# A corrected port flag in the planner of an attention and two-mixer kernel, and a new list of nudges that re-deals its order

## The chip, the cores and the metric

The kernel runs on one core of one Trainium2 chip. A time is the device time of one execution in microseconds (us). The time of a kernel is the median of several executions. The profile shows one execution, instruction by instruction, with the engines PE (TensorE; PEld is its weight load), DVE (VectorE), ACT (ScalarE), POOL (GpSimd) and SP (the queue that issues nearly all DMAs).

## The reference

For 4 batches of 12 heads, 448 tokens and head size 64, the reference computes an attention, a gated mixer and a second mixer, one after the other:

```python
q_n, k_n = (rmsnorm(q, g_q), rmsnorm(k, g_k))
attn = softmax(q_n @ k_n.T / 8); x = attn @ v            # per head, then heads side by side: [4, 448, 768]
h = np.maximum(x @ w_in, 0.0)                            # 768 -> 1024
u, v = h[..., :512], h[..., 512:]
v_s = np.einsum('ts,bsd->btd', w_spatial, norm(v)) + b_spatial[None, :, None]
x = (u * v_s) @ w_out                                    # 512 -> 768
u = x + (np.maximum(x.T @ w_tok1, 0.0) @ w_tok2).T       # over tokens, 448 -> 256 -> 448
out = u + np.maximum(u @ w_ch1, 0.0) @ w_ch2             # 768 -> 1536 -> 768
```

## The kernel before, in words

The program doesn't write its instructions in the order in which they are issued. It first records them. `Plan.add` (from L162) makes an `Op` of every call, with an estimated cost, with the operations it depends on, and with a flag `port`: True where the planner holds that the operation occupies what VectorE and GpSimd share. `Plan.place` is a list scheduler. It walks through time, takes for each engine the waiting operation of the lowest weight, refuses an operation whose flag `port` is set while the other engine's flagged operation runs, prefers TensorE products of the tiling in use over those of another (tilings are 1: contraction over at most 64 rows, 2: at most 64 output rows, 0: neither), and gives PSUM banks to tiles. `Plan.issue` calls it eight times with weights from a backward pass and keeps the best. Then it changes these weights by a long list of seeds, `NUDGES` (L473): every seed moves the weights of a stretch of operations up or down by a pseudo-random amount. The order that comes out is issued (L464 is the line on which all recorded operations are issued, so most rows of the profile bear it). `Plan.warmers` puts throwaway products into a planned TensorE stall of over `IDLE` = 1500 ns (L456).

The work, by the names in the profile:

- Attention goes over 24 pairs of heads. For a pair: `raw` (q and k as loaded, scaled on GpSimd or VectorE by the root mean squares `r...`), `tp` (transposes on TensorE, of `raw`, of the exponentials `e` and of `stage`, a spatial weight), `whole` or `qt`, `kt` (transposed q and k in SBUF), `sc` (scores), `nm` (VectorE's row maxima), `e` (ScalarE's exponentials), `et` (the transposed exponentials, copied from PSUM by ScalarE and VectorE), `av` (the values' product, 64 output rows), `over` (reciprocals of the row sums, which go through DRAM, `over_d`), and `xp`, the pair's result in two parts (upper on ScalarE, rest on GpSimd).
- The first mixer goes over the 4 batches, each after its 6 pairs: `vps` (weights `wv`), `ups` (weights `wu`, written to DRAM once as `wu_d` and loaded again, 768 KB at a time), `sps` (spatial), `xps`.
- The second mixer: `h1ps` and `u_ps` over tokens, then `h2ps` and `o_ps` over channels, each a long row of products.
- Weights come as 64-bit words and are converted on ScalarE, VectorE and GpSimd (`word`, `wpart`).

The first batch's attention has to run before any mixer product is there. Later attention pairs run among mixer products.

Of the kernel before, what the change touches and what calls it, by code (L numbers as in the profile page):

```python
# [152 lines left out]
class Plan:  # L153
# [8 lines left out]
    def add(self, engine, fn, args, kwargs):  # L162
        op = Op()
        op.engine, op.more, op.dma = engine, [], fn == "dma_start"
        op.call = (fn, args, kwargs)
        named = dict(kwargs)
        out = named.pop("out", None)
        rest = list(args)
        if out is None:
            out = rest.pop(0)  # L170
        outs = [x for x in (out, named.pop("accum_out", None)) if isinstance(x, Part)]
        ins = [x for x in rest + list(named.values()) if isinstance(x, Part)]
        op.cost, op.late = self.estimate(engine, fn, out, ins, kwargs)

        sbuf = [x for x in ins if not x.tile.psum]
        op.port = engine == "gpsimd" and bool(sbuf) or engine == "vector" and (
            len(sbuf) > 1 and free(sbuf[1].shape) > 1
            or len(ins) == len(sbuf) and fn in ("tensor_scalar", "tensor_copy"))

        op.parts = 0  # L180
        if engine == "tensor":
            op.parts = 1 if ins[0].shape[0] <= 64 else 2 if out.shape[0] <= 64 else 0
        if self.joined:
            self.joined[0].more.append(op)
            self.joined[0].cost += op.cost
            op = self.joined[0]
        else:
            op.deps = set()
            self.ops.append(op)
        if self.joined is not None:  # L190
            self.joined.append(op)
        for x in ins:
            t = x.tile
            assert t.writers, "read before it is written"
            assert t.make or covered(x, t.writers), "read before all of it is written"
            op.deps.update(w for y, w in t.writers if x.meets(y))
            if t.psum:
                op.deps.update(r for _, r in t.readers if r.engine != engine)
            t.readers.append((x, op))
            t.users.append(op)  # L200
        for x in outs:
            t = x.tile
            before = [w for y, w in t.writers if x.meets(y)]
            if not before:
                self.later.append((op, t.after))
            op.deps.update(before)
            op.deps.update(r for y, r in t.readers if x.meets(y))
            t.writers = [(y, w) for y, w in t.writers if not x.covers(y)] + [(x, op)]
            t.readers = [(y, r) for y, r in t.readers if not x.covers(y)]
            t.users.append(op)  # L210
        op.deps.discard(op)
# [259 lines left out]
SWITCH, NEAR, FAR, EARLY = 300, 2500, 10000, 95000  # L471
NUDGED = 4000
NUDGES = (  # L473
# [21 lines left out]
)  # L495
ENGINES = "gpsimd", "scalar", "sync", "tensor", "vector"
IDLE, SPARE, PACE = 1500, 200, 546
# [33 lines left out]
def covered(x, writers):  # L531

    left = volume(x.box)
    for y, _ in writers:
        left -= volume([(max(a, c), min(b, d)) for (a, b), (c, d) in zip(x.box, y.box)])
    return left <= 0
# [9 lines left out]
def free(shape):  # L546
    n = 1
    for x in shape[1:]:
        n *= x
    return n  # L550
# [11 lines left out]
def attention_moe_mixer(  # L562
# [887 lines left out]
    def up(wp, chan, ut):  # L1450
# [4 lines left out]
        for name, k in PRODUCTS:  # L1455
            w = chan.pop(k, None) or build(wp, c1_d, k)
            for b in range(B // 2):
                op = operand(wp, [P, 2, JH, S], "op", 2, first[b][name])
                for f in range(KH):
# [12 lines left out]
                    if name == "A11":  # L1472
                        nc.scalar.activation(at0(c12), ps, AF.Copy)
                    elif name == "A12":
                        add(c11, c12)
                        relu(c11)
                    elif name == "S2":
                        add(c12, c12)
                    elif name == "S3":
                        add(c21, c12)  # L1480
                    elif name == "S1":
                        add(c22, c21)
                        add(c12, c12)
                        relu(c22)
                    elif name == "S4":
                        add(c12, c12)
                        relu(c12)
                    else:
                        add(c21, c21, ALU.subtract)
                        relu(c21)  # L1490
# [186 lines left out]
```

## Time and profile before

| what | value |
|---|---|
| median of 3 executions | 847.92 us (847.16 to 848.81) |
| the profiled execution's own time | 847.23 us |
| its span, first to last instruction | 845.2 us |
| PE busy | 833.1 us (99%), 5530 records |
| DVE / ACT / POOL busy | 674.7 / 526.7 / 344.6 us |

Some 2.0 us of the time lie around the span. A "busy" PE includes time in which a product streams or drains and the modelled end of a product, so idle PE time by the profile is a lower bound of what TensorE loses. A product of 32-bit numbers leaves two records for one instruction (5530 records for 5255 instructions).

### The profile page before, as it was taken

How to read it: one execution, taken by the hardware profiler on the slowest of the kernel's cores; microseconds unless marked ns; L12 is line 12 of the kernel's file. 1: busy time of each engine (PE TensorE's matmuls, PEld its weight loads, DVE VectorE, ACT ScalarE, POOL GpSimd, SP SyncE). 2: the span in 40 equal slices, each digit the busy share in tenths (PEclk: the TensorE clock that was granted, in tenths of full speed). 3: DMA queues.
4: the chain of work that ended last, by engine and by line, in shares of the span. 5: the costliest groups of instructions: out<-in, count | busy, mean ns of one | idle time of the engine just before them, and what ended most of it. 6: DMA issues, size and time to landing. Idle time of an engine off the chain costs nothing.

```text
span 845.2 us, 16488 instructions
## 1 busy us (share of the span) xinstructions
PE 833.1 (99%) x5530; PEld 700.4 (83%) x5530; DVE 674.7 (80%) x1340; ACT 526.7 (62%) x1268; POOL 344.6 (41%) x431
## 2 busy tenths in 40 slices
PE   7999999999999999999999999999999999999998
PEld 5454567777678876787799999999999999999998
DVE  6899899886787778787475677988889876998863
ACT  6999899897776878766343565554345654343331
POOL 2457555663445524242152222525331018515460
PEclk9999999999999999999999999999999999999999
DMA  6656676766765866466968787667555635742441
GB/s 170 161 160 185 177 232 184 236 169 170 241 184 144 216 171 196 124 180 194 331 201 247 234 275 252 220 197 221 156 175 175 214 123 161 226 140 84 140 142 66
DMA packets 158532, 157.94 MB, mean 187 GB/s; under 512 B 79216, under 2 KB 141616, under 8 KB 158448
## 3 DMA queue, kind: packets, MB, share of 16 engines
q1 hardware_dynamic: 157984, 156.86, 62.1%
q8 instruction: 44, 0.72, 0.4%
q14 instruction: 40, 0.33, 0.1%
q10 hardware_dynamic: 464, 0.03, 0.0%
HBM read 117.95 MB, written 38.88 MB: 186 GB/s over the span
## 4 chain that ended last, share of the span: by engine, by line
PE 82%; ACT 9%; DMA 3%; DVE 3%; issue 1%; SPq 1%; POOL 0%; ACTq 0%; POOLq 0%; DVEq 0%
PE o_ps L464 18%; PE h2ps L464 18%; PE xps L464 7%; PE ups L464 7%; PE av L464 6%; PE vps L464 5%; PE tp L464 5%; PE sc L464 4%; PE sps L464 4%; ACT e L464 4%; PE h1ps L464 4%; PE u_ps L464 3%; ACT et L464 2%; ACT sq L464 1%; DMA raw<-in_k_dram 1%
## 5 line engine op out<-in xcount | busy, mean ns | idle before, releaser
L464 PE MATMUL h2ps<-op,w 128*128 128x448 f32 x756 | 154.1, 366 | 0.0
L464 PEld LDWEIGHTS o_ps<-w,op 128*128 128x128 f32 x900 | 154.0, 188 | 0.0
L464 PE MATMUL o_ps<-w,op 128*128 128x384 f32 (+1 forms) x900 | 153.9, 332 | 0.0
L464 PEld LDWEIGHTS h2ps<-op,w 128*128 128x128 f32 x756 | 141.6, 188 | 11.2
L464 ACT ACTIVATE e<-sc,nm 112x448 f32<-112x448 f32 x184 | 121.7, 692 | 5.5 <-DVE nm L464 5.3
L464 DVE TENSOR_REDUCE nm<-sc 112x1 f32<-112x448 f32 x192 | 110.2, 615 | 8.0 <-PE sc L464 7.3
L464 ACT ACTIVATE op<-c 128x768 fp32r<-128x768 f32 x49 | 41.5, 847 | 83.7 <-PE o_ps L464 77.3
L464 POOL TENSOR_TENSOR src<-src 128x384 f32<-128x384 f32 x48 | 61.2, 1284 | 73.4 <-DMA src<-c_d 56.1
L464 PEld LDWEIGHTS tp<-ident,e 64*128 64x128 f32 (+2 forms) x1120 | 55.5, 139 | 27.4 <-ACT e L464 9.5
L464 ACT ACTIVATE et<-tp 128x448 f32<-128x448 f32 (+1 forms) x144 | 72.7, 560 | 4.9 <-PE tp L464 4.5
L464 DVE TENSOR_SCALAR word<-word 128x256 f32<-128x256 f32 (+5 forms) x132 | 60.5, 462 | 18.4 <-ACT word L464 17.3
L464 DVE SCALAR_TENSOR_TENSOR word<-raw,word 128x256 uint32<-128x256 uint32 (+2 forms) x132 | 71.2, 541 | 1.8
L464 POOL TENSOR_TENSOR u<-u,o 128x384 f32<-128x384 f32 x28 | 40.5, 1464 | 68.4 <-ACT o L464 38.9
L464 PE MATMUL tp<-ident,e 48*128 48x48 f32 (+2 forms) x1120 | 65.4, 232 | 1.2 <-ACT e L464 0.8
L464 PE MATMUL ups<-xp,wu 128*128 128x448 f32 x288 | 65.9, 368 | 0.0
L464 DVE TENSOR_TENSOR op<-c,op 128x768 fp32r<-128x768 f32 x49 | 54.6, 1115 | 10.3 <-ACT op L464 10.3
L464 PE MATMUL av<-et,v 128*64 128x448 f32 x288 | 61.1, 550 | 1.4 <-ACT e L464 0.9
L464 PEld LDWEIGHTS ups<-xp,wu 128*128 128x128 f32 x288 | 53.7, 188 | 6.4 <-ACT e L464 0.7
L464 DVE TENSOR_TENSOR c<-c,h2ps 128x448 f32<-128x448 f32 x84 | 49.7, 613 | 8.4 <-PE h2ps L464 8.2
L464 PE MATMUL xps<-wo,g 128*128 128x384 f32 x288 | 55.1, 340 | 0.0
L464 PE MATMUL sc<-kt,qt 64*112 64x448 f32 x384 | 52.9, 384 | 0.0
L464 PE MATMUL vps<-wv,xp 128*128 128x512 f32 x216 | 52.8, 397 | 0.0
(146 smaller groups left out, 1595.1 us busy)
## 6 DMA issues: line engine op xcount, KB each, us to landing
src<-c_d SPq DMA_DIRECT2D x132, 192.0 KB
wu<-wu_d SPq DMA_DIRECT2D x16, 768.0 KB
wo<-wo_d SPq DMA_DIRECT2D x16, 768.0 KB
raw<-in_moe_w_ch_dram SPq DMA_DIRECT2D x36, 256.0 KB
raw<-in_moe_w_ch_dram SPq DMA_DIRECT2D x24, 384.0 KB
raw<-in_q_dram SPq DMA_DIRECT2D x48, 112.0 KB
over<-over_d SPq DMA_DIRECT2D x48, 112.0 KB
u<-u_d SPq DMA_DIRECT2D x28, 192.0 KB
```

The lines of the kernel that those rows point to most:

```text
L464: getattr(getattr(self.nc, op.engine), fn)(*args, **kwargs)
```

## The change

It alters which operations carry the flag `port`: a VectorE `tensor_tensor` of two SBUF operands now carries it however short its second operand is, and a `tensor_scalar` or `tensor_copy` from SBUF of one element per partition no longer does. It replaces the list `NUDGES` by another, of 267 seeds in place of 228. No operation is added, removed or moved to another engine, and `IDLE`, `SPARE` and `PACE` of the throwaway products stay as they are.

```diff
-            len(sbuf) > 1 and free(sbuf[1].shape) > 1
-            or len(ins) == len(sbuf) and fn in ("tensor_scalar", "tensor_copy"))
+            len(sbuf) > 1 and (fn == "tensor_tensor" or free(sbuf[1].shape) > 1)
+            or len(ins) == len(sbuf) and fn in ("tensor_scalar", "tensor_copy") and free(ins[0].shape) > 1)
...
 NUDGES = (
-    30000007, 30000023, 30000034, 30000042, 30000052, 30000053, 30000068, 30000070, 30000077, 30000078, 30000083,
...
+    30000003, 30000004, 30000005, 30000028, 30000030, 30000033, 30000039, 30000046, 30000048, 30000053, 30000066,
...
 )
 ENGINES = "gpsimd", "scalar", "sync", "tensor", "vector"
 IDLE, SPARE, PACE = 1500, 200, 546
```

What it does to the order, at three places. First TensorE, where the eighth pair's `raw` is transposed, shortly ahead of the first mixer product. Before:

```order
L464 MATMUL av<-et,v_864 64x448 x2
L464 MATMUL tp<-ident,raw 128x112 x8
L464 MATMUL tp<-ident,stage 128x112 x3
L464 MATMUL sc<-whole 112x448 x2
L464 MATMUL tp<-ident,stage 64x112
L464 MATMUL av<-et,vrest 64x448 x2
L464 MATMUL av<-et,v_1125 64x448 x2
```

And now:

```order
L464 MATMUL av<-et,v_952 64x448 x4
L464 MATMUL av<-et,vrest 64x448 x2
L464 MATMUL tp<-ident,e 128x112
L464 MATMUL tp<-ident,raw 128x112 x4
L464 MATMUL tp<-ident,e 128x112 x2
L464 MATMUL tp<-ident,raw 128x112
L464 MATMUL tp<-ident,stage 128x112 x3
L464 MATMUL tp<-ident,raw 128x112 x3
L464 MATMUL tp<-ident,e 128x112 x4
```

The eight transposes of `raw`, which stood in one row, are split by transposes of `e` and `stage`.

Second TensorE again, around the first mixer products `vps` and the values' product `av` that follows them. Before:

```order
L464 MATMUL vps<-wv,xp 128x512 x7
L464 MATMUL tp<-ident,e 128x112 x7
L464 MATMUL sc<-whole 112x448 x2
L464 MATMUL tp<-ident,raw 128x64 x14
L464 MATMUL sc<-whole 112x448 x2
L464 MATMUL av<-et,v_1310 64x448 x6
L464 MATMUL vps<-wv,xp 128x512 x12
```

And now:

```order
L464 MATMUL vps<-wv,xp 128x512 x8
L464 MATMUL tp<-ident,e 128x112 x7
L464 MATMUL vps<-wv,xp 128x512 x8
L464 MATMUL tp<-ident,raw 128x64 x14
L464 MATMUL sc<-whole 112x448 x4
L464 MATMUL av<-et,v_1321 64x448 x4
L464 MATMUL sc<-whole 112x448 x4
L464 MATMUL vps<-wv,xp 128x512 x6
```

Six of the twelve `vps` that stood behind the `av` (5 + 7 were ahead of it, 2 + 8 + 8 are now) have moved ahead of it.

Third the DMA queue SP, at the first load of `wu`, which the first `ups` reads. Before (the queue's row 98 is the load):

```order
L464 DMA raw<-in_k_dram 64x64
L464 DMA raw<-in_k_dram 64x7x64
L464 DMA raw<-in_k_dram 64x6x64
L464 DMA wu<-wu_d_59 128x1536
L464 DMA raw<-in_moe_w_in_dram 128x2x256
L464 DMA wu_d_60<-wpart 256x1x256
```

And now (row 143):

```order
L464 DMA v_1666<-in_v_dram 128x3x64
L464 DMA wu_d_62<-wpart 256x1x256
L464 DMA vrest<-in_v_dram 64x64 x2
L464 DMA wu<-wu_d_59 128x1536
L464 DMA raw<-in_moe_w_out_dram 128x512
L464 DMA v_1666<-in_v_dram 128x3x64
L464 DMA wu_d_62<-wpart 256x1x256
L464 DMA wu<-wu_d_60 128x1536
```

The first load of `wu` now stands behind two writes of the third part of `wu_d` and just ahead of the second load, where it had stood 42 rows ahead of that one.

## Rows read from the trace of the kernel before

**Rows 1.** The page's head, its busy times, and the clock line of its 40 slices.

```profile
span 845.2 us, 16488 instructions
...
PE 833.1 (99%) x5530; PEld 700.4 (83%) x5530; DVE 674.7 (80%) x1340; ACT 526.7 (62%) x1268; POOL 344.6 (41%) x431
...
PEclk9999999999999999999999999999999999999999
```

**Rows 2.** Busy times by stretches: stretch, its length, busy us and records by engine, clock, DMA.

```profile
0.00:21.13 21.13, 15.82 (x98) 12.25 (x99) 12.88 (x33) 13.77 (x34) 6.30 (x24) 1.00 0.69 170
...
21.13:84.52 63.39, 60.33 (x363) 31.70 (x361) 57.44 (x131) 63.39 (x183) 37.26 (x59) 1.00 0.62 169
84.52:126.78 42.26, 41.57 (x278) 25.06 (x278) 38.23 (x104) 36.69 (x105) 22.09 (x34) 1.00 0.70 205
126.78:824.07 697.29, 697.17 (x4681) 613.33 (x4678) 559.32 (x1065) 410.33 (x947) 279.00 (x317) 1.00 0.63 192
...
824.07:845.20 21.13, 18.20 (x118) 18.03 (x117) 6.84 (x11) 2.55 (x3) 0.00 (x0) 1.00 0.19 66
```

**Rows 3.** Pieces of the chain that ended last: start us, us, what, records.

```profile
406.88 14.97 PE vps L464 x66
...
537.30 151.19 PE h2ps L464 x746
688.49 153.79 PE o_ps L464 x900
```

**Rows 4.** Waits of the weight load: who waited for whom, us, times, longest.

```profile
PEld av L464 <- issue: 30.6, 125, 0.7
...
PEld tp L464 <- issue: 8.6, 20, 1.3
PEld sc L464 <- issue: 5.7, 19, 0.7
```

**Rows 5.** Groups of ACT: shapes, count, busy us, mean ns of one, idle before.

```profile
L464 ACT ACTIVATE et<-tp 128x448 f32<-128x448 f32 x96 | 55.5, 592 | 3.8 <-PE tp L464 3.6
...
L464 ACT ACTIVATE xp<-over 128x448 fp32r<-128x448 f32 x24 | 15.2, 635 | 10.7 <-DVE over L464 10.6
...
L464 ACT ACTIVATE ry<-ra 128x14 f32<-128x14 f32 x16 | 3.6, 227 | 2.0 <-POOL ra L464 1.9
L464 ACT ACTIVATE ry<-ry 128x14 f32<-128x14 f32 x16 | 3.6, 227 | 0.4
```

**Rows 6.** Timeline of PE, 83 to 104 us: start us, us, what [idle before <-releaser].

```profile
83.59 0.60 PE L464 MATMUL tp<-ident,raw 112*128 112x112 f32 x4 [0.73 <-POOL raw L464]
84.59 0.60 PE L464 MATMUL tp<-ident,raw 112*128 112x112 f32 x4 [0.40 <-POOL raw L464]
...
94.68 1.39 PE L464 MATMUL vps<-wv,xp 128*128 128x512 f32 x5
...
98.58 1.01 PE L464 MATMUL sc<-whole 64*112 64x448 f32 x4
...
101.34 2.48 PE L464 MATMUL av<-et,v 128*64 128x448 f32 x12 [0.53 <-DVE over L464]
```

**Rows 7.** Loads of `wu` on SP, the first long `ups`, and the DMA of 112 to 125 us.

```profile
80.06 0.61 SPq L464 DMA_DIRECT2D wu<-wu_d  x1
...
115.31 0.61 SPq L464 DMA_DIRECT2D wu<-wu_d  x1
...
131.19 3.62 PE L464 MATMUL ups<-xp,wu 128*128 128x448 f32 x17
...
DMA packets 3026, 3.27 MB, mean 251 GB/s; under 512 B 1920, under 2 KB 2391, under 8 KB 3025
```

**Rows 8.** Throwaway products at the start, by stretches; and PE's longest wait for data.

```profile
1.60:5.20 3.60, 3.60 (x17) 3.60 (x18) 1.00 0.78 171
5.50:6.90 1.40, 1.40 (x15) 1.40 (x14) 1.00 0.70 144
...
9.37 0.60 PE L464 MATMUL tp<-ident,raw 112*128 112x112 f32 x4 [1.60 <-DVE raw L464]
```

44 rows, old and new, of the table NUDGES are left out of this document.

## The prediction
> **What bounds the kernel now.** I read the page first, then the busy times by stretches, then the chain of waits, then the places where TensorE waited. The page says that PE is busy for 833.1 of 845.2 us [rows 1], so 12.1 us of the span hold no product. The stretches say where those lie [rows 2]: 21.13 - 15.82 = 5.31 us in the first 21 us, 63.39 - 60.33 = 3.06 us from 21 to 85 us, 42.26 - 41.57 = 0.69 us from 85 to 127 us, 697.29 - 697.17 = 0.12 us in the 697 us after that, and 21.13 - 18.20 = 2.93 us in the last slice. The reader is to see that from 127 us on TensorE never stops. The second mixer alone is a row of 746 products `h2ps` in 151.19 us, then 900 `o_ps` in 153.79 us, without a gap in the chain [rows 3]. So the kernel is bound by TensorE's work, and an order can only win what lies ahead of 127 us.
>
> From 21 to 85 us a second engine is full: ACT is busy for 63.39 of 63.39 us [rows 2]. There the first pairs' exponentials feed the transposes and value products, and no mixer product can fill in, since `vps` needs the first batch's results. What ScalarE must do ahead of the first `vps` bounds this stretch from below; TensorE's idle 3.06 us are its echo.
>
> **The change, part by part.** *The flags.* No instruction reads them; they act through the order alone. Their direct cost is nothing and nothing has to hide it.
>
> *The work.* Counted in the two orders, every engine issues the same instructions: 5255 on TensorE in both, 1342 on VectorE, 1084 on ScalarE, 433 on GpSimd, 883 on SP. The throwaway products are 16, 1 and 4 in both, at the same three places, so that part of the planner's pass fills nothing new. Cost: 0.
>
> *The ends.* TensorE's first 80 products and its last 1651 stand in the same order in both. The 5.31 us of the first slice and the 2.93 us of the last stay: 0.
>
> *Changes of tiling on TensorE.* I counted in the orders how often a product of one tiling follows one of another: 136 times before and 136 times now. The mix differs: from column tiling to full products 13 before and 5 now, from half rows to full 32 and 38, from column tiling to half rows 24 and 30, the opposite of the last 22 and 20, full to half rows 30 and 28, full to columns 15 and 15. The rows price a stop of the weight load for no visible cause by the product that comes next: 30.6/125 = 0.245 us for `av`, 8.6/20 = 0.43 us for `tp`, 5.7/19 = 0.30 us for `sc` [rows 4]. If all 12 switches that changed kind moved from the cheapest to the dearest, that is 12 x (0.43 - 0.245) = 2.2 us, and as much the other way if they moved back. I take 0, since the total is the same and the rows name the next product, not the kind of switch; 2.2 us either way stays as a bound. The Trainium skill, page "TensorEngine Tiling (Array Packing)", section "Key Properties", says that changing the tiling mode drains TensorE, whichever mode; by that rule 136 switches against 136 cost the same and this term is 0, where the rows would allow 2.2 us.
>
> *ScalarE's work ahead of the first mixer product.* 391 products stand ahead of the first `vps` in both orders. The last exponential that a transpose needs just ahead of it has 184 ACT operations in front of it in both. They differ by four: one more `et` (0.592 us) and one more `xp` (0.635 us), two `ry` fewer (2 x 0.227 us) [rows 5]. That is 0.592 + 0.635 - 0.454 = +0.77 us. ScalarE is full there, so I take all of it; the other end is 0, since PE idles 3.06 us in the stretch and part of the wait can move into that.
>
> *The transposes of the eighth pair.* Before, they waited 0.73 and 0.40 us for GpSimd's scaled `raw`, one half each [rows 6]. Now the second half's first transpose has two transposes of `e` ahead of it, at about 0.1 us each, which cover 0.2 us of the 0.40 us; the first half still follows the value products directly, with one transpose between. GpSimd's row is as before (a `wpart` product, then the two scalings). I take -0.2 us; the ends are -1.13 us (both waits gone) and +0.4 us (GpSimd later by half a scaling).
>
> *The value product behind the first `vps`.* It waited 0.53 us until VectorE had emptied the earlier one's bank [rows 6]. Now six more `vps`, at 14.97/66 = 0.227 us [rows 3], and two more `sc` of the pair that took 1.01 us for two (four records) [rows 6] stand between the two value products: 1.4 + 1.0 us against 0.53 us. The wait goes, -0.53 us. If VectorE's copy is later by as much, it stays: 0.
>
> *SP.* The first load of `wu` stood at row 98 of the queue and stands at row 143. Before, it was issued at 80.06 us for use at 131.19 us; the second load, at row 140 then, was issued at 115.31 us [rows 7]. So the first load will be issued at about 115 us, with some 16 us in hand, and at the stretch's mean rate of 251 GB/s [rows 7] its 768 KB take 3.1 us. Cost 0, covered by the products ahead of the first `ups` (617 before, 599 now); without that cover it is the second rival.
>
> Sum against the profiled execution's own 847.23 us: + 0.77 - 0.2 - 0.53 = +0.04, that is **847.3 us**. The profiled execution lies 0.7 us under the median of the three shown (847.92 us) and inside their range, so I leave the forecast at 847.3 us. It is no change. 0.2% of the time, 1.7 us, is about what a measurement of this kernel can tell from none, so "the same" reaches from 846.2 to 849.6 us.
>
> **The rivals.** *First, the idle time ahead of 127 us goes.* The new order may close half or all of the 3.06 + 0.69 us [rows 2]: 847.3 - 1.9 = 845.4 us at half, 847.3 - 3.75 = 843.6 us at all. For it speaks that both places which I compared have more work in front of the wait. Against it speaks that ACT is full from 21 to 85 us and has as much to do as before ahead of the first `vps`; a wait that TensorE is spared there comes back a few products later. I give it 0.34.
>
> *Second, slower: the first load of `wu` comes too late.* It stands now behind two writes of `wu_d` that wait for GpSimd's `wpart`, and right ahead of the second load. If the queue is held for more than about 16 - 3 = 13 us (less where other loads share the engines, by half the rate 16 - 6 = 10 us), the 18 first `ups` wait, and from there each us is one us of the kernel, less what other products are ready. With 3 us over, that is 850.3 us. Against it: SP issued what stood there at 115 us. Chance 0.11.
>
> *Third, slower: the saturated stretch gets holes.* From 127 us to the end of the attention pairs, ahead of the long row of `vps` at 407 us [rows 3], TensorE lost at most 0.12 us [rows 2]; there the old order has nothing left to win, and a new one can lose. At the rate of the stretch before (0.69 us in 42.26 us) over 280 us, that is 4.6 us; half of it gives 849.6, two thirds 850.3 us. It decides where a batch's mixer products run out before the next batch's pairs are done. Chance 0.11.
>
> *Fourth, the clock.* The granted clock is 1.00 (2.4 GHz) in all 40 slices [rows 1], through a wait of 1.60 us [rows 8] as well, so fewer idle stretches can give no clock back. At the start the products ran slower, 17 in 3.60 us and then 15 in 1.40 us [rows 8], though the column reads 1.00 there too; if a longer idle brought that pace back for as many products, it cost 17 x (3.60/17 - 1.40/15) = 2.0 us: 849.3 us. The Trainium skill, page "TensorE: Matmul & The Clock Gate", section "Why this matters for your kernels", says that a TensorE left idle between bursts falls back to the lower clock; by it a new order could lose time that the old one keeps, and the trace has no stretch that did. Chance 0.04.
>
> That the change doesn't do what it says has in part happened already (no more throwaway products than before), and its time is that of the forecast.
>
> **How the numbers follow.** The forecast has 0.40, and the clock's 0.04 ends within 0.2% too: 0.44 for the same. Faster is the first rival, 0.34. Slower are the second and third, 0.22. The range leaves out about a tenth on each side: it goes into the first rival as far as four fifths of the idle time, 844.3 us, which also holds the 2.2 us of the switches, and up to the two slower rivals' 850.3 us.
>
> **What would show it.** Right: ACT again full from 21 to 85 us and PE idle there 2 to 4 us; the first `vps`, at 94.68 us before [rows 6], between 94 and 96 us; no wait of the value product that follows the first `vps`; PE idle under 0.5 us from 127 us on; the row of 746 `h2ps` starting within 1 us of 537.3 us [rows 3]. The first rival would show as PE idle under 1.9 us between 21 and 127 us, with the first `vps` earlier than 94 us. The second would show as `ups` waiting for a DMA at about 130 us, the third as waits of PE between 127 and 400 us, the fourth as a slice with a lower clock or with products at the doubled interval. Most likely to make the forecast wrong is that small waits inside what counts as busy add up: a tenth of a us at each of the 136 switches is 13.6 us, more than all the idle time that the profile shows.

## The result, and the profile after

The changed kernel takes 852.60 us (median of 8 executions, 849.79 to 855.17), the kernel before 848.01 us beside it (8, 847.16 to 849.67). The ratio is 1.0053, 95% interval 1.0036 to 1.0070: slower by 4.5 us, between 3.1 and 5.9. The forecast was 847.3 us, with a range up to 850.3 us.

The profiled execution took 853.08 us, 5.85 us more than the one before, so it shows about 1.3 us more than the medians differ by. The page's head and busy times, to be set beside [rows 1]:

```profile
span 851.3 us, 16447 instructions
...
PE 834.1 (98%) x5530; PEld 701.6 (82%) x5530; DVE 679.2 (80%) x1340; ACT 527.8 (62%) x1268; POOL 347.8 (41%) x431
```

The span is 6.1 us longer. PE is busy 1.0 us longer and idle 851.3 - 834.1 = 17.2 us instead of 12.1 us, 5.1 us more. Where, the busy times by stretches tell (stretch, its length, busy us and records of PE, PEld, DVE, ACT, POOL, then clock, DMA share and GB/s), beside [rows 2]:

```profile
0.00:21.13 21.13, 15.80 (x88) 11.51 (x89) 11.93 (x31) 12.47 (x31) 5.35 (x23) 0.92 0.68 164
21.13:84.52 63.39, 59.70 (x361) 31.06 (x359) 59.40 (x132) 63.27 (x183) 37.61 (x58) 1.00 0.59 156
84.52:126.78 42.26, 40.44 (x252) 24.07 (x250) 37.79 (x100) 35.56 (x105) 25.27 (x40) 1.00 0.68 202
126.78:210.00 83.22, 83.06 (x762) 64.77 (x761) 63.24 (x151) 69.51 (x194) 44.86 (x71) 1.00 0.70 202
210.00:290.00 80.00, 78.49 (x656) 58.38 (x655) 64.41 (x150) 62.32 (x173) 41.68 (x64) 1.00 0.63 170
290.00:410.00 120.00, 119.43 (x1034) 94.07 (x1035) 91.91 (x232) 86.92 (x236) 36.99 (x56) 1.00 0.63 187
410.00:824.07 414.07, 412.85 (x2240) 393.61 (x2237) 340.83 (x533) 193.50 (x349) 156.07 (x122) 1.00 0.63 196
...
824.07:851.30 27.23, 24.30 (x154) 24.12 (x152) 9.72 (x15) 4.24 (x5) 0.00 (x0) 1.00 0.18 65
```

The same view of the kernel before, with its long stretch cut at the same times:

```profile
126.78:210.00 83.22, 83.22 (x756) 64.61 (x752) 69.50 (x163) 71.77 (x205) 46.28 (x79) 1.00 0.67 189
210.00:290.00 80.00, 80.00 (x668) 61.06 (x668) 62.14 (x151) 61.17 (x170) 39.82 (x63) 1.00 0.67 191
290.00:410.00 120.00, 119.92 (x1010) 91.11 (x1009) 88.32 (x219) 83.86 (x225) 36.84 (x55) 1.00 0.64 188
410.00:824.07 414.07, 414.02 (x2252) 396.54 (x2251) 339.36 (x532) 193.53 (x349) 156.07 (x120) 1.00 0.62 193
```

The new idle time is 0.0 us at the start (5.33 against 5.31), 0.6 from 21 to 85, 1.1 from 85 to 127, 0.2, 1.5, 0.5 and 1.2 us in the four stretches behind that, and 0.0 at the end: 5.1 us. The 1.0 us of busy time belongs to the start, where the granted clock reads 0.92 instead of 1.00: there the first 16 records of `sc` took 4.96 us instead of 3.26 us. The long rows of the second mixer take what they took [rows 3]; they only start later (chain of waits: start us, us, what, records):

```profile
411.55 14.29 PE vps L464 x62
...
543.40 151.18 PE h2ps L464 x746
694.58 153.80 PE o_ps L464 x900
```

`h2ps` starts 6.1 us later, the whole difference of the spans. So nothing is lost behind 543 us. Ahead of that, the view of PE's waits was empty behind 127 us for the kernel before, and has five rows now (who waited for whom: us, times, longest):

```profile
PE tp L464 <- DVE x L464: 0.9, 1, 0.9
PE sc L464 <- DVE over L464: 0.9, 1, 0.9
PE tp L464 <- ACT e L464: 0.5, 1, 0.5
PE av L464 <- ACT et L464: 0.5, 1, 0.5
PE xps L464 <- POOL g L464: 0.3, 1, 0.3
```

Each is one late hand-over. Three of them show how one comes about. The timeline from 273 us on (start us, us, engine, what, [idle before <- releaser]):

```profile
273.82 1.83 POOL L464 TENSOR_TENSOR raw<-raw,ry 128x384 f32<-128x384 f32 x2
...
275.61 1.35 POOL L464 TENSOR_TENSOR xp<-over,xp 128x448 fp32r<-128x448 f32 x1
276.99 1.09 SPq L464 DMA_DIRECT2D over<-over_d  x2
...
280.35 0.62 DVE L464 TENSOR_TENSOR over<-av,over 128x448 f32<-128x448 f32 x1 [1.07 <-DMA over<-over_d]
...
281.03 0.46 PE L464 MATMUL sc<-kt,qt 64*112 64x448 f32 x2 [0.86 <-DVE over L464]
```

GpSimd scales two halves of `raw` that TensorE transposes only at 297.7 us, and only then makes `xp`, which frees the buffer into which the next `over` is loaded. So SP issues that load at 276.99 us, VectorE stands 1.07 us at the head of its queue until it lands, and the scores wait for the PSUM bank that VectorE empties. VectorE waited for that kind of load for 0.7 us before, and for 4.3 us now (waits of DVE from 20 to 824 us; before, then after):

```profile
DVE over L464 <- DMA over<-over_d: 0.7, 2, 0.5
```

```profile
DVE over L464 <- DMA over<-over_d: 4.3, 5, 1.1
```

At 339 us it is ScalarE, whose `word` waits for a weight load ahead of an eviction that a value product needs:

```profile
338.75 0.43 ACT L464 ACTIVATE word<-raw 128x256 f32<-128x256 f32 x1 [1.25 <-DMA raw<-in_moe_w_ch_dram]
339.08 0.87 ACT L464 ACTIVATE et<-tp 128x448 f32<-128x448 f32 x2
...
339.66 1.72 PE L464 MATMUL av<-et,v 128*64 128x448 f32 x8 [0.48 <-ACT et L464]
```

At 541 us it is VectorE, whose `word` takes 1.77 us while GpSimd products run, where such a one takes 0.54 us on average, with the sum into `x` behind it:

```profile
539.02 1.77 DVE L464 TENSOR_SCALAR word<-word 128x384 uint32<-128x384 uint32 x1
539.56 2.08 POOL L464 TENSOR_TENSOR src<-src 128x384 f32<-128x384 f32 x2
...
540.71 0.54 DVE L464 TENSOR_TENSOR x<-u_ps,x 64x384 f32<-64x384 f32 x1
...
541.31 0.44 PE L464 MATMUL tp<-ident,x 128*128 128x128 f32 x2 [0.88 <-DVE x L464]
```

```profile
L464 DVE TENSOR_SCALAR word<-word 128x384 uint32<-128x384 uint32 x24 | 12.9, 539 | 0.3
```

The last row is the group of these instructions (count, busy us, mean ns of one).

### The profile page after: what moved, and what is told of

It is laid out like the page before. It is cut to its first block, busy times and chain, and to the rows that moved or that the text cites. A ratio compares the mean times of both kernels' runs of the same rounds, so it can differ in the third digit from the quotient of the medians.

```text
span 851.3 us, 16447 instructions
## 1 busy us (share of the span) xinstructions
PE 834.1 (98%) x5530; PEld 701.6 (82%) x5530; DVE 679.2 (80%) x1340; ACT 527.8 (62%) x1268; POOL 347.8 (41%) x431
## 4 chain that ended last, share of the span: by engine, by line
PE 80%; ACT 5%; DMA 5%; POOL 3%; SPq 3%; DVE 3%; issue 2%; POOLq 0%; DVEq 0%; ACTq 0%
PE o_ps L464 18%; PE h2ps L464 18%; PE ups L464 7%; PE xps L464 6%; PE vps L464 5%; PE av L464 5%; PE tp L464 5%; PE sc L464 4%; PE sps L464 4%; PE u_ps L464 4%; PE h1ps L464 4%; SPq L464 3%; ACT e L464 2%; ACT et L464 1%; DMA raw<-in_k_dram 1%
## 5 line engine op out<-in xcount | busy, mean ns | idle before, releaser
L464 ACT ACTIVATE e<-sc,nm 112x448 f32<-112x448 f32 x184 | 119.2, 672 | 5.0 <-DVE nm L464 4.5
L464 DVE SCALAR_TENSOR_TENSOR word<-raw,word 128x256 uint32<-128x256 uint32 (+2 forms) x132 | 73.7, 563 | 2.0
L464 ACT ACTIVATE et<-tp 128x448 f32<-128x448 f32 (+1 forms) x144 | 69.2, 545 | 5.2 <-PE tp L464 4.9
L464 PE MATMUL tp<-ident,e 48*128 48x48 f32 (+2 forms) x1120 | 67.2, 233 | 1.8 <-ACT e L464 0.9
L464 PEld LDWEIGHTS xps<-wo,g 128*128 128x128 f32 x288 | 50.0, 188 | 2.5 <-POOL g L464 0.7
```

The source lines that it names most:

```text
L464: getattr(getattr(self.nc, op.engine), fn)(*args, **kwargs)
```

## Experiments

In what follows the lag of a product is its start less the sum of the usual intervals of all products ahead of it, worked out from a trace; differences in us are the recorded ratio of the two kernels' times, with its interval, times 848.2 us; it lies within 0.05% of the ratio of the medians.

**Whose stretch loses.** Eight kernels hold both orders and issue the work that one plan starts in its first so many us, then the rest in the order of the other (`PARTS`: port rule and table, 0 for old and 1 for new, and the time in ns). A PSUM tile keeps its planned bank where that is free, and takes the longest free one where it isn't. For the first:

```diff
+PARTS = ((0, 0, 20000), (1, 1, None))
...
+        for rule, seeds, until in PARTS:
+            start, bank, warm, _ = made[rule, seeds]
+            order = sorted(range(len(ops)), key=lambda i: (start[i], i))
+            if until is not None:
+                order = [i for i in order if start[i] < until]
+            for i in order:
+                if i not in done:
+                    done.add(i)
+                    todo.append((i, bank, warm.get(i, ())))
```

> Splice: the order of the kernel before for all that its plan starts in the first 20 us, then the rest in the order of the changed kernel; same work, 136 changes of TensorE's tiling. Theory A (each hole belongs to the order of its own stretch; in the changed kernel's profile the products' lag grows by 1.3 us more than before up to 20 us, 0.8 from 20 to 127 and 3.5 from 127 on): 852.6 - 1.3 = 851.3, some 1.7 lower still if the clock's dip at the start goes with it. Theory B (the late start alone sets off all later holes): 848.0, the time of before.

> The mirror: the changed kernel's order for the first 20 us of its plan, then that of before. Theory A: 848.0 + 1.3 = 849.3, up to 851.0 if the clock's dip costs another 1.7. Theory B: 852.6, the time of the changed kernel.

> Before's order up to 127 us of the plan, the changed kernel's from there (138 tiling changes). Theory A: 848.0 + 3.5 = 851.5, from the idle 3.5 us against 0.1 of TensorE behind 127 us. Theory B: 848.0. Should the holes behind 127 us come from work that the first 127 us left late, 848 too.

> The changed kernel's order up to 127 us, before's from there (136 tiling changes). Theory A: 848.0 + 1.3 + 0.8 = 850.1, up to 851.8 with the clock's dip. Theory B: 852.6.

> Seam at 210 us of the plan, where the plan itself shows no hole at the seam (the four splices so far had some): before's order up to there, the changed kernel's behind it. Theory A (the holes belong to the order of their own stretch; in the two profiles the lag of the changed kernel's products grows by 3.0 us more than before's behind 210 us): 848.2 + 3.0 = 851.2. Theory C (before's order has so few holes only as a whole, and any other order has holes along its whole length): 851 to 853 too. Theory D (all comes from the start and the first 127 us): 848.2.

> Seam at 290 us, no hole at it in the plan. Theory A: behind 290 us the lag grows by 0.4 us more than before's (less from 300 to 400, 1.5 more from 400 on): 848.6. Theory C: 851 to 853. Theory D: 848.2.

> The changed kernel's order up to 160 us, before's behind it, no hole at the seam in the plan. Theory A: 1.0 us from 20 to 160, with up to 1.3 for the start: 849.2 to 850.5. Theory C: 851 to 853. Theory D: 852.6.

> The changed kernel's order up to 400 us, before's behind it, no hole at the seam in the plan. Theory A: the lag is 4.7 us larger at 400 us, 1.3 of it at the start: 851.6 to 852.9, and no wait of a product for x at 541 us. Theory C: 851 to 853. Theory D: 852.6.

| order | median, us | against before, us |
|---|---|---|
| before to 20, then after | 852.71 | +4.7 (3.6 to 5.9) |
| after to 20, then before | 851.28 | +2.6 (1.4 to 3.8) |
| before to 127, then after | 856.21 | +7.9 (6.5 to 9.2) |
| after to 127, then before | 852.10 | +3.8 (2.8 to 4.8) |
| before to 210, then after | 850.81 | +2.2 (1.3 to 3.1) |
| before to 290, then after | 848.00 | -0.3 (-1.1 to +0.5) |
| after to 160, then before | 851.56 | +3.1 (2.0 to 4.3) |
| after to 400, then before | 851.76 | +3.1 (2.0 to 4.1) |

The first four fit no theory well: before's first 20 us help nothing (against B, and against a loss at the start), and the pairs of halves lose more than the whole, 7.3 and 11.7 us against 4.5. The seam is to blame at least in part. Behind the seam at 127 us the third order's transposes waited 0.28 and 1.41 us, and TensorE ran slower after that: twelve records of `sc` took 2.58 us, and eleven a little later 1.45 us; the stretch from 140 to 150 us reads a clock of 0.83, where both whole orders read 1.00.

```profile
140.26 0.77 PE L503 MATMUL tp<-ident,raw 64*128 64x64 f32 x13 [1.41 <-ACT et L503]
```

```profile
140.00:150.00 10.00, 9.64 (x93) 8.01 (x95) 7.96 (x19) 9.14 (x28) 6.37 (x10) 0.83 0.70 197
```

The next four have seams that the plan passes without a hole. On the chip such a seam isn't always free: "after to 160" has 1.58 us of idle time between 160 and 210 us, where before's whole order has none. Behind 290 us the changed order costs nothing by the times, against C (every other order loses along its length); behind 210 us it costs 2.2 us, against D (all comes from the first 127 us). "After to 160" takes 851.56 us, over the 849.2 to 850.5 us of theory A and inside those of C, and "after to 400" lies where A and C both put it. So no theory holds for all eight. Step by step from the end, the loss is 0 behind 290 us, 2.2 + 0.3 = 2.5 us from 210 to 290 us, and 4.5 - 2.2 = 2.3 us ahead of 210 us. Step by step from the start it is 3.1 us up to 160 us, 0 from 160 to 400 us, and 4.5 - 3.1 = 1.4 us behind that. Each of these steps is uncertain by a us or more, and the two ways don't agree; that the loss adds up stretch by stretch is not shown.

The rows say more clearly where TensorE waits. In the stretch from 210 to 290 us (busy times as above) PE has holes with the seam at 210 and none with the seam at 290, which has before's order there.

```profile
210.00:290.00 80.00, 79.45 (x651) 60.22 (x650) 59.66 (x147) 60.21 (x166) 40.30 (x63) 1.00 0.64 179
```

```profile
210.00:290.00 80.00, 80.00 (x666) 60.62 (x665) 63.96 (x154) 61.58 (x169) 39.86 (x60) 1.00 0.65 188
```

Behind 410 us TensorE is idle for 1.22 to 1.25 us wherever the changed order stands there (the changed kernel and the first, third, fifth and sixth splice), each time with the wait of 0.9 us for `x`; wherever before's order stands there (before and the other four) it is idle for 0.05 us at most, as the last of the expectations had it. So that wait belongs to the order of its own stretch. "Before to 290" against "after to 400":

```profile
290.00:410.00 120.00, 118.83 (x1013) 92.10 (x1013) 88.16 (x220) 83.62 (x227) 36.75 (x56) 1.00 0.63 187
410.00:824.07 414.07, 412.84 (x2243) 395.14 (x2242) 342.04 (x531) 193.59 (x349) 153.91 (x122) 1.00 0.62 194
```

```profile
410.00:824.07 414.07, 414.02 (x2250) 396.34 (x2249) 341.24 (x533) 193.69 (x349) 155.96 (x120) 1.00 0.63 195
```

This goes against a loss of nothing behind 290 us: the profiled execution of "before to 290" lost 1.17 + 1.23 = 2.4 us there and took 849.53 us, 1.5 us over the median of that kernel. A single profile does not say what the median loses.

**Waits taken away by hand.** The planned order with single instructions put elsewhere in their engine's queue: six moves against five waits in the changed kernel (the numbers are the planner's), three against two in the one before:

```diff
+MOVES = ((712, 485), (1004, 918), (2827, 2224), (2826, 2224), (2937, 3372), (4823, 4824))
...
+        order = sorted(range(len(ops)), key=lambda i: (start[i], i))
+        for i, j in MOVES:
+            order.remove(i)
+            order.insert(order.index(j), i)
...
+MOVES = ((862, 634), (863, 634), (880, 881))
```

> The changed kernel with five instructions (or their neighbours) put elsewhere in their engine's queue, each ahead of a wait that its profile shows: at 74 us POOL scales raw before it makes xp; at 101 us xp before the second half of raw; at 274 us xp before both halves of raw (so that the buffer of over comes free and its load starts); at 339 us ScalarE's copy of word, which waits for a load, behind two evictions of et; at 539 us VectorE's copy of word behind the sum into x. Theory H (the loss is made of such waits, one by one): the five last 0.88 + 0.7 + 0.86 + 0.63 + 0.88 = 3.95 us, so 852.6 - 4.0 = 848.6. Rival (TensorE is late for what stands behind those waits, and the next wait takes up what one gives back): 851.5 or more.

> The kernel before with the same kind of edit: at 82 us POOL scales both halves of raw before a piece of wpart (wait of the transposes 0.73 us), at 100 us VectorE's sum into over stands ahead of a piece of wpart (wait of av 0.53 us). Theory H: 848.2 - 1.2 = 847.0. Rival: 848.2.

The changed kernel with moves took 850.81 us, +1.9 us against before (0.7 to 3.0) where it was +4.5: it got back 2.6 of the 4.0 us, about two thirds, and lies between theory H and the rival, nearer to H. (By the rows shown, the second and fourth of the five waits are 1.25 and 0.48 us long, not 0.7 and 0.63.) In its profile PE is idle for 849.3 - 833.8 = 15.5 us, 1.7 us less, and only 0.6 us of that lies behind 127 us. Its waits of PE there say why not more:

```profile
PE tp L470 <- ACT e L470: 1.2, 2, 0.8
PE tp L470 <- DVE tv L470: 0.6, 1, 0.6
PE tp L470 <- ACT et L470: 0.4, 1, 0.4
PE xps L470 <- POOL g L470: 0.3, 1, 0.3
```

The waits for `x` (0.9), for `over` (0.9) and of `av` for `et` (0.5) are gone; three others have come, 0.42, 0.62 and 0.83 us, at 227, 279 and 343 us. So the five waits can be taken away, and time comes back; how much of it belongs to each of them is not shown, as they went together and the order behind them shifted. The kernel before with moves took 849.77 us, +0.4 us (-0.4 to +1.4): of its 1.2 us nothing came back. Of its two waits at 84 us the first went and the second stayed, `av` still waited for `over`, and TensorE was idle for 0.44 and 0.38 us at 91 and 94 us, where it had not been.

**The rule, the table, or any order.** One kernel takes the new rule with the old table (the two lines of the rule as in the change above), one the old rule with a table of 33 numbers found from nothing:

```diff
 NUDGES = (
-    30000007, 30000023, 30000034, 30000042, 30000052, 30000053, 30000068, 30000070, 30000077, 30000078, 30000083,
...
+    70000001, 70000011, 70000028, 70000040, 70000058, 70000232, 70000262, 70000278,
...
```

> The new port rule with the old table of numbers: the table was found under the old rule, so under the new one it deals another order, with 149 changes of tiling and, by the planner's own reckoning, 5.9 us more than before (851.95 against 846.08 us in the plan). If the plan's reckoning holds on the chip: 848.2 + 5.9 = 854. If an order that was not picked on the chip loses some 4 us beyond its plan, as the changed kernel does: 858.

> A third order, dealt by the kernel before with its old port rule and a table of 33 numbers that was searched from nothing for the plan's span alone: 845.66 us in the plan (before 846.08, changed kernel 845.76), 133 changes of tiling against 136 and 136. Theory C (an order that was found in the plan alone takes 4 to 7 us more than its plan on the chip, and before's 2.1 us is the exception): 850 to 852.5. If the changed kernel is the exception and plans hold to 2 us: 847.8. If the port rule matters, so that orders planned under the old one do well: 847.8 as well.

The rule alone gave 857.52 us (two executions), +8.3 us (6.4 to 10.3): 5.9 us by the plan's own reckoning, the rest beyond it. The fresh table gave 858.99 us, +10.3 us (8.6 to 12.0), worse than any theory had it, with a plan as short as the other two. In two of its six executions, at a mean granted clock of 0.998, it took 855.7 and 856.1 us; in the other four the clock was 0.991 to 0.994, at 857.8 to 860.4 us. In its profiled execution of 856.10 us PE is idle for 16.8 us, 4.7 us more than before, and busy for 837.1 us, 4.0 us more. The rule alone shows a like split, 17.2 us idle and 837.4 us busy. So neither the new rule nor the changed table is needed for a loss: an order with the shortest plan of the three loses most. Plans that agree within 0.5 us end 11 us apart on the chip, so the plan's span can't rank orders at this level.

**Room for late hand-overs.** Both tables were continued; a number was kept if it shortened the mean of three replays of the fixed order in which hand-overs come up to 0.1 us and transfers up to 0.4 us late.

The kernels differ by these numbers alone; of the 42 and the 20 the first ones:

```diff
+    73000028, 73000181, 73000272, 73000442, 73000573, 73000846, 73000969, 73001330,
...
+    72000026, 72000096, 72000139, 72000327, 72000724, 72001143, 72001346, 72001617,
...
```

> The changed kernel with 42 more numbers behind its table, each taken because it shortened the mean of three replays of the fixed order in which every hand-over between engines comes up to 0.1 us and every transfer up to 0.4 us later than the planner assumes: 847.35 us in such replays against 848.73 for the changed kernel, 844.86 against 845.76 in the plan itself, 133 changes of tiling. If the loss is lateness that the plan leaves no room for: 852.6 - 1.4 = 851.2 or less. If an order's loss on the chip has nothing to do with that: 852 to 854.

> The same for the kernel before: 20 more numbers behind its table, 848.72 us in the replays against 849.11, 846.10 against 846.08 us in the plan, 136 changes of tiling. If lateness in the plan's sense decides: 848.2 - 0.4 = 847.8. Theory C (before's order is an exception and any new deal of it falls back to what orders usually lose): 850 to 852.

The changed kernel took 851.27 us, +3.1 us (1.9 to 4.2) instead of +4.5 (3.1 to 5.9), the 1.4 us expected; the two intervals overlap. The kernel before took 847.65 us beside 848.50 us, -1.1 us (-1.9 to -0.3): the only version here that is faster than both, and a new deal of before's table that loses nothing, against theory C. Its long stretches are full to the last row (busy times as above):

```profile
126.78:410.00 283.22, 283.22 (x2449) 216.64 (x2446) 223.27 (x536) 219.54 (x604) 125.81 (x198) 1.00 0.65 187
410.00:824.07 414.07, 414.07 (x2254) 397.19 (x2253) 334.15 (x535) 193.64 (x349) 155.07 (x120) 1.00 0.63 195
```

Before's had been nearly full there already, and its idle time in all is 846.1 - 833.8 = 12.3 us against 12.1: where its 1.1 us came from the profile doesn't show. The gains are of the size of the intervals, so that they are so near to the replays' is no proof of the replays' numbers. Across families the replays don't rank either: 848.73 us for the changed kernel against 849.11 us for before.

## Why the prediction was wrong

**The step that failed** is the one that put the stretch behind 127 us at nothing: the sum has no term for it. The prediction saw that "the old order has nothing left to win, and a new one can lose" there, made it the third rival, and gave it 0.11. By the profile 3.34 of the 5.1 us of new idle time lie in that stretch (3.46 against 0.12 us); by the times, the changed order behind 210 us, with its seam, costs 2.2 us (1.3 to 3.1). The rival's size was near: it priced 2.3 to 4.6 us for the stretch up to 407 us, and the rows show 2.24 us from 127 to 410 us. Another 1.22 us lie behind 410 us, where no rival looked for it. Its mechanism is not what the rows show. It had a batch's mixer products run out; the rows show five single waits, each behind one late hand-over to the product that came next in TensorE's fixed order, and at 217 us `vps` products stand on both sides of the wait (18 from 207.25 us, 24 from 220.40 us). Whether ready products stood behind the other waits no row says. A forecast from three places, out of an order that was dealt anew everywhere, left out the other places.

**The part ahead of 127 us** was priced at +0.04 us and costs some 2 to 3 us: 2.3 us ahead of 210 us or 3.1 us (2.0 to 4.3) ahead of 160 us by the splices; in the profile 0.6 + 1.1 us of idle, and 1.0 us of busy time at the start. Its terms one by one:

- Flags and work: 0 holds. Counts are equal and every splice does the same work; the flags act through the order alone.
- The ends: idle time stayed at 5.3 and 2.93 us. The first slice's clock did not stay (below): the sum put it at nothing.
- Changes of tiling: as many as before, and nothing that loses here goes with their number: the fresh table has 133 and is the slowest.
- ScalarE ahead of the first `vps`: +0.77 us was priced; the first `vps` came at 96.17 us instead of 94.68, outside the 94 to 96 us that were given, 1.49 us later. The `sc` products that ran at 20.64 us before run at 21.91 us now, so 1.27 us of that are there at 20 us already, ahead of the term that was priced. PE's idle 3.69 us and a full ACT are as forecast.
- The transposes of the eighth pair: both waits went, the lower end (-1.13) and not the -0.2 taken. But an earlier pair's transposes waited instead, at 76.64 us for 0.88 us, behind a GpSimd product on `raw` that took 1.98 us; the prediction has no term for that place.
- The value product behind the first `vps`: its wait went, as forecast. A `vps` in the row ahead of it waited instead, for an `xp` that GpSimd made behind two halves of `raw` and a piece of `wpart`:

```profile
103.00 0.49 PE L464 MATMUL vps<-wv,xp 128*128 128x512 f32 x1 [1.25 <-POOL xp L464]
```

- SP and the second rival: right. The first load of `wu` was issued at 114.0 us and the first `ups` ran at 132.3 us without a wait.

**The first rival**, idle time closed ahead of 127 us, held the largest chance of a gain (0.34) and went the other way. Both places which I compared did improve, as it said; others paid for them.

**The fourth rival**, the clock, is there but is small. The changed kernel's first stretch reads 0.92 after a wait of 2.60 us, where before read 1.00 after 1.60 us [rows 8]. The Trainium skill, page "TensorE: Matmul & The Clock Gate", section "Why this matters for your kernels", has idle between bursts drop the clock, and this trace agrees with that direction. The length of the wait alone does not decide it here: 0.83 followed waits of 0.28 and 1.41 us in the third splice (above), and before's 1.60 us left 1.00. The priced 2.0 us are near to what the 16 records of `sc` lost in this execution, 1.7 us; part of that came back in the next wait, 0.30 us instead of 1.12. Over 85 executions of the kernel before beside the experiments little is left of it: 39 with a mean clock of 1.000 took 848.4 us on average and 46 with a lower one 848.8 us. Nor is it a matter of this order: of the splices with before's first 20 us, those at 20, 127 and 290 us read 0.92 in the first slice and the one at 210 us 1.00; of those with the changed one's, the ones at 127 and 400 us read 0.92, the ones at 20 and 160 us 1.00.

**The last remark** of the prediction, that small waits inside the busy time add up, was not what happened in the changed kernel: 5.1 of the 6.1 us are visible idle time, in waits that are mostly 0.2 to 1.3 us long. In the fresh table and the rule alone it may be a part of it: there 4.0 and 4.3 us lie inside PE's busy time.

What stays open: why the fresh table loses 10 us, of which there is no profile at the lower clock; how the 4.5 us are shared out between the stretches, on which splices and profiles disagree; and whether any new deal of the changed order would have got back as much as the moves did, for the continued table got back 1.4 us.

## What to carry to other kernels

Where a scheduler deals a whole order anew, forecasts from a few compared places are worth little: the question is how much the old order had left to win (here 3.75 us between 21 and 127 us) and how much a typical order loses, and a stretch without idle time has no idle time to give back. A saturated engine with a fixed order stands still at a late hand-over, and what it lost comes back only where a later wait shrinks. So look for what stands at the head of the helpers' queues: a copy that waits for a load, a product that nobody needs for 22 us ahead of one that frees a buffer. If orders are searched in a model, time several candidates (searching with room for lateness came with gains of 1.4 and 1.1 us here, the first not clear of noise); a shorter plan alone says nothing at the level of a few us.

## What the runs showed of the hardware

- A VectorE instruction took longer while GpSimd ran, and a GpSimd product while VectorE ran: the `tensor_scalar` of 128 x 384 from one SBUF operand at 539 us took 1.77 us (mean 0.54 us), and the product on `raw` of 112 x 512 ahead of 76.6 us took 1.98 us (mean 1.17 us). That the one engine held the other is likely, but no run tests it. The Trainium skill, page "GPSIMD Engine Reference", section "Specifications", names contention with VectorE instructions with two SBUF inputs or in a two-port mode; that a one-operand instruction is held too agrees with it if that one runs in such a mode, which no row shows.
- The first loads landed at times that differ by up to 0.8 us between executions, and by 0.5 and 0.7 us under one order of the start: ScalarE's first square started at 5.32 us before and at 5.36 and 5.82 us in two splices with before's first 20 us, at 6.13 us after and at 5.42 us in a splice with the changed order's first 20 us.
- The same work in another order read a mean granted clock of 0.991 to 0.994 in four of six executions (the fresh table; the other two read 0.998), where all other kernels here read 0.995 or more. Why is not shown.
- TensorE's clock fell after short waits at one place and stayed through a longer one at another: 0.83 from 140 to 150 us in the third splice, behind waits of 0.28 and 1.41 us, and 1.00 through 1.60 us in the kernel before [rows 8].
